# Attention rows of every second group left to VectorE in three parts, the first tap weights issued ahead of the weight loads, and the last tiles in twos

## The chip, the cores and the metric

The kernel runs on one core of a Trainium2 chip. A core has a matrix engine (TensorE; in the profile PE, with its weight loads as PEld), a vector engine (VectorE, DVE), an activation engine (ScalarE, ACT), a general engine (GpSimd, POOL) and a queue engine (SyncE, SP), each with its own instruction stream, which it runs in order. They meet through semaphores. The metric is the device time of one execution in microseconds.

## What is computed

Two things in a row, over 8 sequences of 4160 positions with 192 features, in float32. First a causal convolution whose seven taps are made per position and head by a softmax:

```python
w = np.exp(weight_gen - np.max(weight_gen, axis=-1, keepdims=True))
w = w / (np.sum(w, axis=-1, keepdims=True) + 1e-09)       # (B, S, 8 heads, 7 taps)
x_unf = x_pad[:, idx, :].reshape(B, S, K, H, group)       # the 7 last positions of each
out = np.einsum('bshk,bskhg->bshg', w, x_unf)
```

Then every position's 192 values go through a block with 1024 hidden values:

```python
h = x @ w_in
e = np.exp(h - np.max(h, axis=-1, keepdims=True))
sm = e / (np.sum(e, axis=-1, keepdims=True) + 1e-09)
solu = h * sm
ln = (solu - mean) / np.sqrt(var + 1e-06) * g_ln          # mean and var over the 1024
return (ln @ w_out).astype(np.float32)
```

## The kernel before, in words

Partition p holds a run of 260 consecutive positions, so the work is 260 **tiles**, tile t being position t of all 128 runs. Tiles are loaded in chunks (4, 8, then 16 tiles each; `starts`), and attention is made by GpSimd in **groups** of four tiles (the first four in two groups of two), 66 groups in all.

Per chunk, `softmax_taps` makes the tap weights in seven steps t0 to t6 that alternate between engines: VectorE L112 (maximum), GpSimd L114, ScalarE L118 (exponential), VectorE L120 (sum), ScalarE L122, VectorE L124 (reciprocal), GpSimd L126. For the first chunk these seven stand, in program order, behind the issues of the weights' loads (L191 to L207).

Per group, `attention` on GpSimd multiplies the seven shifted rows with the taps (L174), adds products 0 to 2 and 3 to 5 (L180), and then makes two half sums out of the four rows left (L182) into the tile `half`. VectorE adds the two halves (`last_sum`, L433, called "fin" in the order of issue), ScalarE copies 64 columns (L439).

Per two tiles, TensorE transposes (L450, "xT"), ScalarE rounds to the high part (L458, "xhi"), VectorE subtracts for the low part (L479, "xld").

Per tile the chain is: first product on TensorE (L491 and L494, "mm1") into one of three PSUM tiles `h`; VectorE's maximum (L505, "max"); ScalarE's exponential (L509, "exp"); VectorE's product h*e (L515, "solu"); ScalarE's high half in float16 (L528, "hi") and squares with their sum (L521, "sq"); VectorE's low half (L532, "lo"); a transposing DMA on SP's queue (L540, "tr"); the second product on TensorE (L580, "mm2", 24 matmuls) into `po`; ScalarE's scaled copy out (L591, "out"). "sq" and "lo" of one tile read the same `h` and are kept apart: whichever is issued first is waited for by the other. Per two or four tiles (`stat_group`) six small steps f0 to f5 (L555 to L571) make the scale of the output from the statistics.

At the start the double-precision weights are converted on VectorE and ScalarE (`float_of_double`, L241 to L260), w_in as parts a0, b and a1, then w_out as c0 to c3, whose column sums TensorE makes (L342) after ScalarE has scaled them (L334); L292 and L363 are two more small sums. The first product needs the w_in parts, the second those of w_out (L360, L385, L390).

The instruction streams are written out by `issue_order`, a planner in the program: it gives every step a cost, an engine, and a key (its tile number plus a number from the table `URGENCY`), fills the engines one step at a time, and the order in which it placed the steps is the program order. On the chip only the order remains; no time of the planner's is in it.

## Time and profile before

| | us |
|---|---|
| median of 3 runs | 1347.44 (1345.54 to 1348.4) |
| the profiled execution | 1347.67 |
| its span, first to last instruction | 1345.8 |
| TensorE / GpSimd busy | 1246.8 / 1247.7 |
| VectorE / ScalarE busy | 1210.2 / 1162.8 |
| GpSimd's last instruction ends at | 1290.4 |

Between the profiled execution's time and its span lie 1.9 us. A row of the view by stretch gives the stretch in us from the span's start, its length, and then each engine's busy time in it, with the number of instructions; after them come the granted TensorE clock (1.00 is full), the mean busy share of the DMA engines and GB/s. A row of the timeline gives start, duration, engine, line, operation, the tiles out<-in with their shapes, and in brackets how long the engine stood idle before it and for whom. A row of the groups gives line, engine, operation, tiles, shapes out<-in and count, then busy us and mean ns of one, then idle time before. A row of the waits gives who waited for whom: us in total, times, longest.

### The profile page before, as it was taken

The numbers are of one execution on the slowest core, as the hardware profiler recorded it, in microseconds if no ns is written. First come the engines' busy times: TensorE is split into PE (matmuls) and PEld (weight loads), VectorE is DVE, ScalarE is ACT, GpSimd is POOL, SyncE is SP. The second block draws the span as 40 slices with busy tenths as digits, with TensorE's granted clock in tenths as the row PEclk, the third lists the DMA queues.
The fourth block names the chain that finished last, engine by engine and source line by source line (L and its number), as shares of the span: only waits on it lengthen the run. The fifth ranks groups of instructions, "written<-read, shape, count | busy, mean of one in ns | idle before, by whom it ended". The sixth has DMA issues, their size and how long they took to land.

```text
span 1345.8 us, 25810 instructions
## 1 busy us (share of the span) xinstructions
PE 1246.8 (93%) x9900; PEld 970.8 (72%) x9900; DVE 1210.2 (90%) x1588; ACT 1162.8 (86%) x2318; POOL 1247.7 (93%) x241
## 2 busy tenths in 40 slices
PE   0588899999999999999999999999999999999997
PEld 0365677777777777777777777777777777777776
DVE  5988899999999999999999999999999999889994
ACT  3778889889898988989898998989898898988886
POOL 5989899999999999999999999999999999999930
PEclk9899999999999999999999999999999999999999
DMA  5277668797886889688797968878787877976776
GB/s 180 74 159 169 139 134 201 123 207 137 155 179 134 196 137 208 125 179 163 129 202 140 191 140 180 162 128 203 140 193 137 183 150 138 183 134 123 133 134 130
DMA packets 565307, 210.31 MB, mean 156 GB/s; under 512 B 544456, under 2 KB 545864, under 8 KB 565184
## 3 DMA queue, kind: packets, MB, share of 16 engines
q1 hardware_dynamic: 563208, 206.55, 75.7%
q10 hardware_dynamic: 1976, 2.12, 0.6%
q8 instruction: 78, 1.28, 0.4%
q14 instruction: 45, 0.37, 0.1%
HBM read 46.15 MB, written 25.56 MB: 53 GB/s over the span
## 4 chain that ended last, share of the span: by engine, by line
ACT 43%; DVE 35%; issue 11%; PE 7%; DMA 2%; POOL 1%; SPq 0%; ACTq 0%; POOLq 0%
ACT hl L528 12%; ACT e L521 12%; DVE h L515 11%; DVE hl L532 11%; ACT e L509 9%; DVE stats L505 5%; DVE a L433 4%; ACT junk L145 3%; PE po L580 3%; PE h L494 2%; ACT x_hi L458 2%; ACT ot L591 2%; DMA hlT<-hl 2%; PE h L491 1%; DVE x_lo L479 1%
## 5 line engine op out<-in xcount | busy, mean ns | idle before, releaser
L174 POOL TENSOR_TENSOR pr<-xt,wt 128x5376 f32<-128x5376 f32 (+1 forms) x66 | 631.6, 9569 | 2.7
L580 PE MATMUL po<-w_hl,hlT 128*128 128x192 f16 x6192 | 555.1, 246 | 17.3 <-ACT ot L591 12.6
L580 PEld LDWEIGHTS <-hlT 128*128 128x128 f16 x6240 | 505.9, 98 | 83.2 <-issue 75.5
L515 DVE SCALAR_TENSOR_TENSOR h<-h,row,e 128x1024 f32<-128x1024 f32 x260 | 333.8, 1285 | 19.1 <-ACT e L509 16.9
L528 ACT ACTIVATE hl<-h 128x1024 f16<-128x1024 f32 x260 | 266.0, 1029 | 98.4 <-DVE h L515 55.4
L532 DVE SCALAR_TENSOR_TENSOR hl<-h,hl 128x1024 f16<-128x1024 f32 x260 | 316.5, 1218 | 36.8 <-ACT e L521 34.4
L180 POOL TENSOR_TENSOR pr<-pr 128x2304 f32<-128x2304 f32 (+1 forms) x66 | 333.0, 5045 | 5.2
L505 DVE TENSOR_REDUCE stats<-h 128x1 f32<-128x1024 f32 x260 | 316.3, 1217 | 3.9 <-PE h L494 3.3
L509 ACT ACTIVATE e<-h,stats 128x1024 f32<-128x1024 f32 x260 | 293.3, 1128 | 16.1 <-DVE stats L505 15.5
L521 ACT ACTIVATE e<-h,stats 128x1024 f32<-128x1024 f32 x260 | 293.0, 1127 | 1.1 <-DVE hl L532 1.0
L494 PE MATMUL h<-wa_hi,x_hi 128*128 128x512 f32 x520 | 234.0, 450 | 0.0
L182 POOL TENSOR_TENSOR half<-pr 128x1536 f32<-128x1536 f32 (+1 forms) x66 | 225.8, 3421 | 5.2
L494 PE MATMUL h<-wa_lo,x_hi 128*128 128x512 f32 x520 | 206.4, 397 | 0.0
L494 PE MATMUL h<-wa_hi,x_lo 128*128 128x512 f32 x520 | 205.9, 396 | 0.0
L494 PEld LDWEIGHTS h<-wa_hi,x_hi 128*128 128x128 f32 x520 | 98.1, 189 | 107.1 <-issue 95.5
L491 PE MATMUL h<-wb_hi,x_hi 64*128 64x512 f32 x520 | 131.0, 499 | 17.1 <-DVE hl L532 11.2
L433 DVE TENSOR_REDUCE a<-half 128x768 f32<-128x1536 f32 (+1 forms) x66 | 117.2, 1776 | 0.0
L591 ACT ACTIVATE ot<-po,stats 128x192 f32<-128x192 f32 x258 | 112.4, 436 | 3.6 <-PE po L580 3.6
L494 PEld LDWEIGHTS h<-wa_hi,x_lo 128*128 128x128 f32 x520 | 98.4, 189 | 23.2
L494 PEld LDWEIGHTS h<-wa_lo,x_hi 128*128 128x128 f32 x520 | 99.0, 190 | 12.0
L491 PE MATMUL h<-wb_hi,x_lo 64*128 64x512 f32 x520 | 104.2, 395 | 0.0
L450 PE MATMUL pa<-ident,a 128*128 128x128 f32 x520 | 81.2, 278 | 23.9 <-DVE x_lo L479 13.2
(89 smaller groups left out, 1072.0 us busy)
## 6 DMA issues: line engine op xcount, KB each, us to landing
out_dram<-ot SPq DMA_DIRECT2D x65, 384.0 KB, 3.3
xt<-in_x_dram SPq DMA_DIRECT2D x30, 576.0 KB, 4.8
xt<-in_x_dram SPq DMA_DIRECT2D x30, 480.0 KB, 4.4
wt<-in_weight_gen_dram SPq DMA_DIRECT2D x15, 448.0 KB, 4.8
hlT<-hl SPq DMA_TRANSPOSE x260, 4.7
xt<-in_x_dram SPq DMA_DIRECT2D x3, 384.0 KB, 4.6
raw_a<-in_moe_w_in_dram ACTq DMA_DIRECT2D x2, 512.0 KB, 7.4
raw<-in_moe_w_out_dram ACTq DMA_DIRECT2D x1, 768.0 KB, 12.2
```

The source lines that it names most:

```text
L174: nc.gpsimd.tensor_tensor(out=window(pr, 0, [(TG * D, K), (HG, n * H), (1, HG)]), in0=window(xt, t * D, [(D, K), (HG, n * H), (1, HG)]), i ...
L180: nc.gpsimd.tensor_tensor(out=pr[:, :3], in0=pr[:, :3], in1=pr[:, 3:6], op=ALU.add)
L182: nc.gpsimd.tensor_tensor(out=half, in0=window(pr, 0, [(2 * TG * D, 2), (D, n), (1, D)]), in1=window(pr, TG * D, [(5 * TG * D, 2), (D, n), ...
L491: nc.tensor.matmul(h[:, fs], lhs[rows, 1, :], rhs[rows], start=n == 0, stop=False)
L494: nc.tensor.matmul(h[:, fs], lhs[:, 0, :], rhs[:, fs], start=False, stop=n == 2)
L505: nc.vector.tensor_reduce(stat(t, NMAX), h_of[t], axis=AX.X, op=ALU.max, negate=True)
L509: nc.scalar.activation(e, h_of[t], AF.Exp, bias=stat(t, NMAX), accum_out=stat(t, Z))
L515: nc.vector.scalar_tensor_tensor(out=h, in0=h, scalar=row(t, SCALE), in1=e, op0=ALU.mult, op1=ALU.mult, accum_out=stat(t, M))
L521: nc.scalar.activation(e_of.pop(t), h_of[t], AF.Square, bias=stat(t, M), scale=-float(FF), accum_out=stat(t, Q),)
L528: nc.scalar.activation(hl[:, 0, :], h_of[t], AF.Copy, scale=2.0**14)
L532: nc.vector.scalar_tensor_tensor(out=hl[:, 1, :], in0=h_of[t], scalar=2.0**14, in1=hl[:, 0, :], op0=ALU.mult, op1=ALU.subtract,)
L580: nc.tensor.matmul(po[:, :D], hlT[:, half * NJ + j, :], w2_hl[:, j, w, :], start=n == 0, stop=n == len(terms) - 1,)
```

## The change

Four things change in the code. (1) For a group whose number t // 4 is odd, `half` has three parts: GpSimd's first addition writes them (products 0 to 2 plus 3 to 5), the seventh product is added to the first of them in place, the addition into two halves is gone, and VectorE's `last_sum` reduces over three parts. There are 32 such groups, all of four tiles; the others are as before. `half` grows from two to three parts in both its buffers. (2) The seven tap steps of the first chunk are issued directly behind the loads of its x and taps, ahead of the weights' loads. (3) The last four tiles are attended to, and get their output scales, in twos. (4) The planner has other costs for the three-part groups, other times at which engines and data are taken to be free, one more precedence for the scaling of w_out (parts a0 and a1 are converted first), and a new table `URGENCY`, so that the order of nearly all instructions on all engines is another.

```diff
@@ def attention(xt, wt, t, n, half):
+        if half.shape[1] == 3:
+            nc.gpsimd.tensor_tensor(out=half, in0=pr[:, :3], in1=pr[:, 3:6], op=ALU.add)
+            nc.gpsimd.tensor_tensor(out=half[:, 0], in0=half[:, 0], in1=pr[:, 6], op=ALU.add)
+            return
         nc.gpsimd.tensor_tensor(out=pr[:, :3], in0=pr[:, :3], in1=pr[:, 3:6], op=ALU.add)
...
     load_x(0)
+    for step in range(TAP_STEPS):
+        softmax_taps(0, step)
     raw_a = att.tile([P, 2 * FF], I32, name="raw_a", bufs=1)
...
-
-    for step in range(TAP_STEPS):
-        softmax_taps(0, step)
...
     def stat_group(t):
-        n = 2 if t < 2 * TG else TG
+        n = 2 if t < 2 * TG or t >= RUN - TG else TG
...
     def group(t):
-        if t < TG:
+        if t < TG or t >= RUN - TG:
             return 2 if t % 2 == 0 else 0
         return TG if t % TG == 0 else 0
+
+    def parts(t):
+        return 3 if t // TG % 2 else 2
...
-        half = att.tile([P, 2, TG, D], F32, name="half", bufs=2)[:, :, :n]
+        half = att.tile([P, 3, TG, D], F32, name="half", bufs=2)[:, : parts(t), :n]
...
 URGENCY = dict(
-    a00=3.1, a01=2.3, a02=-28.9, a03=-6.5, a04=-3.6, a10=80, a11=-25.4, a12=-13, a13=-10, a14=10.4,
+    a00=-3, a01=-149.1, a02=7.4, a03=1.4, a04=4.5, a10=-41, a11=-136.7, a12=-13.9, a13=-118.7,
...
-    free = [3000, 5900, 5000, 12000, 9050]
+    free = [3000, 5600, 7700, 12000, 6200]
...
-            once(f"q{f}0", ACT, 700, part + "2")
+            once(f"q{f}0", ACT, 700, part + "2", "a02", "a12")
...
-        add("attA", t, POOL, 14990 if full else 7500, *after, ready=15000 if c == 1 else 9000)
-        add("attB", t, POOL, 3510 if full else 1800, ("attA", t), ("fin", groups[i - 2] if i > 1 else -1))
+        three = t // 4 % 2
+        add("attA", t, POOL, (9790 if three else 14990) // (1 if full else 2), *after, ready=21500 if c == 1 else 10000)
+        add("attB", t, POOL, (6950 if three else 3510) // (1 if full else 2), ("attA", t), ("fin", groups[i - 2] if i > 1 else -1))
...
-        add("fin", t, DVE, 1710 if full else 880, ("attB", t), ("xT", old + 2 if old >= 0 else -1))
+        add("fin", t, DVE, (2500 if three else 1710) // (1 if full else 2), ("attB", t), ("xT", old + 2 if old >= 0 else -1))
```

In the changed file the lines up to L174 keep their numbers; the two new additions are L181 and L182, the old two are L184 and L186; the loads are six lines lower down (L195 is L201), the weights' preparation three (L342 is L345), and the lines of the tile chain seven (L494 is L501, L521 is L528, L528 is L535).

The new table moves instructions at three places that the prediction speaks of. The first is ScalarE's stream at the start: `xt`, `raw_a` and `raw_2` are the tiles into which x, w_in and w_out are loaded, `wt` the taps, `junk` the squares of x. Before:

```order
L79 DMA xt<-in_x_dram 15x1152 x4
L195 DMA raw_a<-in_moe_w_in_dram 128x1024 x2
L202 DMA raw<-in_moe_w_out_dram 128x4x384
L206 DMA g<-in_moe_g_ln_dram 128x8x1
L118 ACTIVATE wt<-wt 128x224
L145 ACTIVATE junk,squares_x<-xt 128x1920
L122 ACTIVATE wy<-wm 128x32
```

And in the changed kernel:

```order
L79 DMA xt<-in_x_dram 15x1152 x4
L201 DMA raw_a<-in_moe_w_in_dram 128x1024
L118 ACTIVATE wt<-wt 128x224
L201 DMA raw_a<-in_moe_w_in_dram 128x1024
L122 ACTIVATE wy<-wm 128x32
L208 DMA raw<-in_moe_w_out_dram 128x4x384
L212 DMA g<-in_moe_g_ln_dram 128x8x1
```

ScalarE's two tap steps (L118, L122) now stand between the DMA issues, the second load of w_in and that of w_out behind them.

The second is TensorE's stream up to the third tile's first product (`pa` is written by the transposes, `po` by the sums over the weights, `h` by the first products; of each first product only its first row is shown here). Before:

```order
L292 MATMUL po<-sq,ones 128x3
L450 MATMUL pa<-ident,a 128x128 x4
L342 MATMUL po<-raw_a,ones 128x192 x2
L450 MATMUL pa<-ident,a 128x128 x4
L342 MATMUL po<-raw_a,ones 128x192 x2
L491 MATMUL h<-wb_hi,x_hi 128x512 x2
```

And in the changed kernel:

```order
L457 MATMUL pa<-ident,a 128x128 x4
L295 MATMUL po<-sq,ones 128x3
L457 MATMUL pa<-ident,a 128x128 x4
L345 MATMUL po<-raw_a,ones 128x192 x4
L498 MATMUL h<-wb_hi,x_hi 128x512 x2
```

Before, the sums of the first and of the second part of w_out stood ahead of the first tile's first product, in two pieces with a transpose between; now one row of four matmuls (two parts' sums) stands there, behind both transposes.

The third is ScalarE's stream in the middle of the program, tiles 170 to 172 before and 162 to 163 in the changed kernel (the numbers tell the buffers apart: an `h_` number is one tile). Before:

```order
L528 ACTIVATE hl_10506<-h_10401 128x1024
L521 ACTIVATE e_10472,stats_139<-h_10401,stats_139 128x1024
L509 ACTIVATE e_10516,stats_139<-h_10459,stats_139 128x1024
L591 ACTIVATE ot_10420<-po_10480,stats_139 128x192
L458 CAST x_hi_10534<-pa_10511 128x512
```

And in the changed kernel, the same steps seven lines higher:

```order
L535 ACTIVATE hl_10008<-h_9895 128x1024
L516 ACTIVATE e_10012,stats_139<-h_9956,stats_139 128x1024
L598 ACTIVATE ot_10028<-po_9980,stats_139 128x192
L562 ACTIVATE stats_139<-stats_139,row_7916 128x4
L528 ACTIVATE e_9969,stats_139<-h_9895,stats_139 128x1024
```

The squares of a tile (L521, now L528) stood right behind its high half and ahead of the next tile's exponential; here they stand behind the next exponential and the copy out. Both patterns occur in both programs. Of the 260 rows of the squares, 67 wait on VectorE before and 120 in the changed kernel, that is, they are issued behind the tile's low half there.

More of the change, by code (lines that the diff above doesn't have):

```diff
@@ L645 @@
 URGENCY = dict(
-    a00=3.1, a01=2.3, a02=-28.9, a03=-6.5, a04=-3.6, a10=80, a11=-25.4, a12=-13, a13=-10, a14=10.4,
-    attA=85.1, attB=2.4, b0=120.9, b1=-144.6, b2=138.3, b3=-1.5, b4=54.3, c00=-28.1, c01=85.1,
-    c02=6.8, c10=-25.3, c11=31.3, c12=-72.7, c20=99.4, c21=-5.6, c22=10.2, c30=-149.7, c31=-14.5,
-    c32=-100.3, dup=52.6, exp=-129.5, f0=8.2, f1=-120.4, f2=-71.5, f3=-118.4, f4=-66.1, f5=-45.6,
-    fin=18.4, hi=-11, lo=33, lw=18.7, lx0=10.2, lx1=-115.4, lx2=-109.1, lx3=-20.7, max=-30,
-    mm1=25.5, mm2=0.4, n0=-7.5, n1=11.8, n2=-1.8, n3=-113.6, n4=-8.6, n5=-69, n6=-123.6, od=-6.9,
-    out=-81.2, p30=22.9, p31=0.5, p4=9.7, p5=12.6, p6=11.6, p70=-10.2, p71=-8.7, p80=20.3, p81=5.9,
-    q00=7.1, q01=-5.1, q02=118.9, q10=-15.7, q11=20.7, q12=16.8, q20=100.6, q21=-95.2, q22=20.4,
-    q30=143.8, q31=81.5, q32=98.3, solu=-7.6, sq=5, t0=5.1, t1=-3.7, t2=77.9, t3=44.1, t4=-26.5,
-    t5=110.1, t6=267.2, tr=-13, v00=170.9, v01=5.1, v02=44, v03=0.2, v1=54.2, v2=58.8, v3=-12.2,
-    v4=1, v5=21.2, xT=-66.9, xhi=-46.7, xld=30,
+    a00=-3, a01=-149.1, a02=7.4, a03=1.4, a04=4.5, a10=-41, a11=-136.7, a12=-13.9, a13=-118.7,
+    a14=8, attA=78.6, attB=-30.7, b0=-73.2, b1=-107.9, b2=10.9, b3=64, b4=76.6, c00=-59.4,
+    c01=91.8, c02=-77.6, c10=-126.1, c11=133.9, c12=-2, c20=4.6, c21=-22.1, c22=-33.2, c30=-2.8,
+    c31=148.3, c32=20.6, dup=-30.2, exp=-265.5, f0=-7.8, f1=-33.1, f2=-75.4, f3=-322.6, f4=44.3,
+    f5=-45.6, fin=17.5, hi=2.4, lo=-96.1, lw=-6.9, lx0=23.5, lx1=0.2, lx2=-19.1, lx3=-15.4,
+    max=2.6, mm1=-3.4, mm2=1.7, n0=257, n1=-49.4, n2=31.3, n3=-114.7, n4=124.6, n5=-8.5, n6=12.5,
+    od=140.5, out=-181.5, p30=107.4, p31=-13.9, p4=-46, p5=84.1, p6=-11.6, p70=-18.2, p71=-102.8,
+    p80=24.2, p81=3.6, q00=2.2, q01=-34.7, q02=15.8, q10=-168.8, q11=44.9, q12=31.7, q20=-7.6,
+    q21=7.5, q22=-1.3, q30=24.6, q31=1.8, q32=-121, solu=-2.8, sq=72.9, t0=13.8, t1=28, t2=87.6,
+    t3=96.9, t4=138.5, t5=-1.5, t6=-141.4, tr=-155.6, v00=7.3, v01=168.7, v02=106.5, v03=46.2,
+    v1=11.3, v2=-84.2, v3=81.7, v4=108.9, v5=-190.2, xT=-6.4, xhi=63.8, xld=0.8,
 )
@@ L682, in issue_order @@
         w_in, size = n < 3, 512 if n < 3 else 384
-        at = (9000, 10500, 12000)[n] if w_in else 15000
+        at = (12000, 12000, 12500)[n] if w_in else 20000
         before = () if w_in else (f"{parts[n - 3]}4", "n" + {"a0": "0", "a1": "1", "b": "2"}[parts[n - 3]]) if n < 6 else ("q00",)
@@ L732, in add_norms @@
         add("v5", t, ACT, 240, ("v4", t))
-    add("v00", 0, ACT, 1800, ready=9000)
+    add("v00", 0, ACT, 1800, ready=10000)
     add_norms(0, 0)
@@ L751, in issue_order @@
             else:
-                add(f"v0{part}", t, ACT, size, ready=15000)
+                add(f"v0{part}", t, ACT, size, ready=21500)
         add_norms(c, t)
```

## The prediction

> **What bounds the kernel now.** I read the page's engine totals first, then busy time by stretch, cut where tiles 0, 16, 48, 256 and 259 begin their first product.
>
> ```profile
> PE 1246.8 (93%) x9900; PEld 970.8 (72%) x9900; DVE 1210.2 (90%) x1588; ACT 1162.8 (86%) x2318; POOL 1247.7 (93%) x241
> ...
> 45.84:138.56 92.72, 71.82 (x475) 52.81 (x474) 80.20 (x113) 73.41 (x154) 87.86 (x19) 0.91 0.63 138
> 45.84:299.99 254.15, 226.03 (x1716) 172.88 (x1716) 227.68 (x303) 217.49 (x439) 241.39 (x48) 0.97 0.73 150
> 922.57:1000.41 77.84, 75.88 (x609) 59.13 (x608) 72.26 (x94) 69.85 (x140) 76.59 (x15) 1.00 0.78 163
> 1233.49:1309.86 76.37, 75.67 (x610) 59.61 (x610) 69.50 (x90) 66.42 (x126) 56.23 (x10) 1.00 0.74 133
> 299.99:1323.30 1023.31, 1000.43 (x8013) 780.41 (x8012) 944.40 (x1217) 915.59 (x1812) 976.18 (x177) 1.00 0.79 158
> 1323.30:1345.80 22.50, 14.95 (x157) 13.34 (x156) 7.71 (x11) 10.01 (x21) 0.00 (x0) 1.00 0.48 108
> ```
>
> No single engine owns the span. In the steady part 16 tiles take 77.84 us; of these TensorE is busy 75.88, GpSimd 76.59, VectorE 72.26, ScalarE 69.85. Two engines are full at once, so I look at who really waits, in the same 16 tiles.
>
> ```profile
> DVE stats L552 <- ACT e L521: 2.5, 3, 1.1
> DVE hl L532 <- ACT e L521: 2.3, 4, 0.6
> DVE h L515 <- ACT e L509: 1.0, 2, 0.8
> ...
> 943.68 3.47 POOL L182 TENSOR_TENSOR half<-pr 128x1536 f32<-128x1536 f32 x1
> 947.62 1.77 POOL L126 TENSOR_TENSOR wt<-wt,wy 128x896 f32<-128x896 f32 x1 [0.46 <-DVE stats L552]
> 951.01 1.80 DVE L433 TENSOR_REDUCE a<-half 128x768 f32<-128x1536 f32 x1
> ```
>
> VectorE takes up a half sum 3.9 us after GpSimd has written it (947.15 to 951.01) and never idles for it; GpSimd, in turn, waits once in 16 tiles, 0.46 us, for VectorE's part of the taps. So GpSimd's own pace is 77.84 - 0.46 = 77.4 us, a hair faster than what the others make, and not what they wait for. The others pace themselves: VectorE waits 5.8 us in 16 tiles (the three rows), always for ScalarE, 4.8 of it for squares (L521), and passes the delay on to TensorE, which loses 77.84 - 75.88 = 1.96. Three levels follow for 16 tiles: TensorE's 75.9 is the floor, GpSimd's 77.4 a second floor close to the time now, and the VectorE-ScalarE exchange sets the 77.8.
>
> The start is looser: tile 48 begins at 299.99, while 48 tiles at 77.84/16 = 4.865 us after 45.84 would have brought it to 279.4. That is 20.6 us lost beside the 45.84 that pass before the first product. After the last first product begins, 22.5 us follow.
>
> **The change part by part.** *GpSimd's additions.* Prices:
>
> ```profile
> L180 POOL TENSOR_TENSOR pr<-pr 128x2304 f32<-128x2304 f32 x64 | 327.7, 5121 | 5.0
> L182 POOL TENSOR_TENSOR half<-pr 128x1536 f32<-128x1536 f32 x64 | 222.2, 3471 | 5.0
> L182 POOL TENSOR_TENSOR half<-pr 128x768 f32<-128x768 f32 x2 | 3.6, 1814 | 0.2
> L433 DVE TENSOR_REDUCE a<-half 128x768 f32<-128x1536 f32 x64 | 115.3, 1801 | 0.0
> L433 DVE TENSOR_REDUCE a<-half 128x384 f32<-128x768 f32 x2 | 1.9, 954 | 0.0
> ```
>
> A three-part group costs 5.12 + 1.81 instead of 5.12 + 3.47: 1.66 us less, 3.3 per 16 tiles, 53 us over 32 groups. That lowers GpSimd's floor from 77.4 to 74.1, under TensorE's 75.9. By itself it is worth nothing in the steady part, since nobody there waits for GpSimd; it takes a ceiling off the order. *VectorE's reduction.* 768 more elements cost 1801 - 954 = 847 ns in the trace, so three parts cost 2.65 us: 0.85 more per group, 1.7 per 16 tiles, 27 us in all, on an engine that has 5.6 us of idle time per 16 tiles, which is not free time but waiting.
>
> *The new order in the steady part* is the unknown. Busy VectorE becomes 72.26 + 1.7 = 73.96. Lower end: TensorE's 75.9 (VectorE would have to wait under 2 us). Upper end: all 5.6 idle us stay and the additions come on top, 79.5. What lies between turns on the squares: low half and squares of a tile exclude each other, and the changed order puts the low half first in 120 tiles against 67. The price of a low half that waits is
>
> ```profile
> DVE hl L532 <- ACT e L521: 34.4, 55, 2.1
> ```
>
> 0.63 us, so 53 tiles fewer spare 33 us in 16.25 chunks' worth of tiles, 2.0 per 16: 73.96 + 5.6 - 2.0 = 77.5. The longer reductions stand mostly right ahead of a low half in the new order and fill part of what that one waits anyway; I give them 0.4 and take 77.1, nearer to today's 77.84 than to either end. The stretch from tile 48 to tile 259 is 211 tiles, 13.2 sixteens: 13.2 x (77.84 - 77.1) = 9.8 us. Its last part already ran at 76.37 per 16, so I count **-8.5**; ends 13.2 x 75.9 = 1002 against 1023.3, -21, and 13.2 x 79.5 = 1049, +26.
>
> A rule of the Trainium skill speaks against my floor: its page Perfetto Trace Analysis, section Identifying the Most-Contended Engine, holds that matmul busy time does not tell how near the roofline TensorE is, and that busy weight loads do. By that reading TensorE is at 59.13 of 77.84 and VectorE's 73.96 would be the floor, 13.2 x 1.9 = 25 us lower than mine. The trace does not bear it out: in a stretch without any idle time, first product to first product takes 4.48 us with no transpose in it (the rows follow), so that 16 tiles cannot go faster than 71.7 plus eight transposes.
>
> ```profile
> 907.53 0.50 PE L491 MATMUL h<-wb_hi,x_hi 64*128 64x512 f32 x2
> ...
> 909.92 2.15 PE L580 MATMUL po<-w_hl,hlT 128*128 128x192 f16 x24
> 912.01 0.50 PE L491 MATMUL h<-wb_hi,x_hi 64*128 64x512 f32 x2
> 916.39 0.60 PE L450 MATMUL pa<-ident,a 128*128 128x128 f32 x4
> ```
>
> (Eight transposes at about 0.53, from the row's 0.60 less the overlap with the next product, make it 75.9 again.)
>
> *The first taps.* Before, GpSimd stood for 13.26 us, because VectorE's sum over the taps was queued behind a conversion that waited for its load until 12.38, and ScalarE's exponential behind five DMA issues.
>
> ```profile
> 8.86 0.39 ACT L118 ACTIVATE wt<-wt 128x224 f32<-128x224 f32 x1 [6.84 <-issue]
> 9.15 1.79 ACT L145 ACTIVATE junk<-xt 128x1920 f32<-128x1920 f32 x1
> ...
> 12.38 0.69 DVE L241 TENSOR_SCALAR h<-raw_a 128x512 int32<-128x512 int32 x1 [9.09 <-DMA raw_a<-in_moe_w_in_dram]
> ...
> 17.08 0.58 POOL L126 TENSOR_TENSOR wt<-wt,wy 128x224 f32<-128x224 f32 x1 [13.26 <-DVE wy L124]
> 17.73 4.95 POOL L174 TENSOR_TENSOR pr<-xt,wt 128x2688 f32<-128x2688 f32 x1
> ```
>
> Now the taps are ready at about 9 and x is there by 9.15 (L145 reads all of it): GpSimd begins 8.5 us earlier. Nothing else waits for GpSimd then: the first two tiles' reduction sits behind the conversions on VectorE, so what counts is VectorE. Moved with the taps: on ScalarE the second load of w_in and that of w_out are issued behind two tap steps, about 1 us later; w_in's second half is read at 21.6 and has 9 us of slack.
>
> VectorE's rows at the start, with ScalarE's scaling and TensorE's sums behind the conversions:
>
> ```profile
> 21.61 0.68 DVE L241 TENSOR_SCALAR h<-raw_a 128x512 int32<-128x512 int32 x1
> 22.33 0.69 DVE L244 TENSOR_SCALAR h<-raw_a 128x512 int32<-128x512 int32 x1
> ...
> 43.38 0.55 DVE L241 TENSOR_SCALAR h<-raw 128x384 int32<-128x384 int32 x1
> 43.96 0.56 DVE L244 TENSOR_SCALAR h<-raw 128x384 int32<-128x384 int32 x1
> ...
> 42.90 0.73 ACT L334 ACTIVATE raw_a<-h,g 128x192 f32<-128x192 f32 x2 [1.36 <-DVE h L260]
> ...
> 44.42 1.49 PE L342 MATMUL po<-raw_a,ones 128*128 128x192 f32 x4
> 45.84 0.79 PE L491 MATMUL h<-wb_hi,x_hi 64*128 64x512 f32 x2
> ```
>
> VectorE from 12.4 us on, counted off its new order: 24 conversions and sums of 512 columns at 0.60 to 0.70, 12 of 384 at 0.56, two reductions at 0.87, two low parts at 0.60, taps 1.6, small ones 0.3, 27.5 us, so the second part of w_out is converted at 39.9. ScalarE scales it (0.73), TensorE sums it (half of the 1.49), and tile 0's product begins near 41.4 instead of 45.84. Four parts are then converted by 47.4, when VectorE begins the first maximum, instead of 50.59.
>
> ```profile
> 50.59 1.21 DVE L505 TENSOR_REDUCE stats<-h 128x1 f32<-128x1024 f32 x1
> ...
> 62.40 1.25 PE L450 MATMUL pa<-ident,a 128*128 128x128 f32 x4 [9.29 <-DVE stats L552]
> 63.58 0.79 PE L491 MATMUL h<-wb_hi,x_hi 64*128 64x512 f32 x2
> 70.04 0.50 PE L491 MATMUL h<-wb_hi,x_hi 64*128 64x512 f32 x2
> ```
>
> TensorE then stands, as it did for 9.29 us before, until VectorE has reduced tiles 4 to 7 and the first tile's low half has freed an `h` for tile 2. From 47.4, VectorE has two maxima, two products, one reduction of 2.65, two operations of 1 us, some small ones and the low half to do: 12 us, 59.4, against 63.58. The fourth tile follows the second low half, near 62, where it began at 70.04 behind a second product that the new order puts later: -8. From there to tile 48 it took 299.99 - 70.04 = 230 us for 45 tiles, which at 4.865 are 219, so 11 us are lost to filling the pipeline. GpSimd, 8.5 us earlier and 1.66 shorter every second group, no longer has its part in these; I take half, 5, and get **-13**; ends 0, if the earlier tiles meet the same later waits, and -19.
>
> *The end.* Twos instead of fours let two tiles' scales be made ahead of the last two's, and the new order keeps seven instead of five second products behind the last first product, where TensorE is idle 22.5 - 14.95 = 7.5 us. Worth 0 to 2 x 2.15 = 4.3 (the L580 row above); the path there is the last tile's own chain and transpose, so **-1.5**.
>
> Sum: -13 - 8.5 - 1.5 = -23 against the profiled execution's 1347.67, which is 0.2 us from the median of 1347.44: 1324.5, forecast **1324**.
>
> **The rivals.** *VectorE becomes the pacer* (slower). The 0.85 us of each longer reduction go onto the chain VectorE-ScalarE-VectorE and no wait shrinks: 79.5 per 16, +26, start -8, no gain at the end: 1347.7 + 26 - 8 = 1366. For it: VectorE's idle time is waiting, not room. Against: fewer low halves behind squares. It decides from the point where VectorE still waits over 77.84 - 73.96 = 3.9 us in 16 tiles. *TensorE goes dense* (75.9): -21 - 19 - 4 = 1304. For it: the tap-free stretch at the end ran at 76.37. Against: VectorE at 73.96 may wait 1.9 only. *Only the start gains*, the steady 77.84 stays: 1347.7 - 13 - 1.5 = 1333. *The change does not do what it says*: the head start is eaten by the wait for `h` and the steady part stays: 1347. *VectorE is the floor and TensorE gives way*: 73.96 per 16, -21 - 25 - 19 - 4 = 1279; the dense rows above speak against it.
>
> **How the numbers follow.** Forecast 0.51, with its own range 1310 to 1338; TensorE dense 0.15; start only 0.14; VectorE as pacer 0.14; no change 0.04; below TensorE's floor 0.02. A measurement of this kernel can tell about 0.2% from no change, 2.7 us. Faster: 0.51 + 0.15 + 0.14 + 0.02 = 0.82; same 0.04; slower 0.14. The range 1300 to 1350 leaves out the pacer's case, the one below the floor and a little of the dense one, about 0.18.
>
> **What would show it.** The first L174 near 9 us and tile 0's product near 41; VectorE's reductions of 128x2304 at 2.65 us and GpSimd's second addition of 128x768 at 1.8; GpSimd now waiting for VectorE, by some 3 us per 16 tiles; 16 tiles in the middle in 76 to 78 us with TensorE still near 75.9 busy. I am wrong if 16 tiles take 78 or more with VectorE waiting as long for L528 (the squares) as before, or if the reductions cost clearly more than 2.65.

## The result, and the profile after

The changed kernel took 1365.2 us (median of four runs, 1361.4 to 1368.2) against 1347.9 us for the kernel before (four runs, 1345.5 to 1348.4): the ratio is 1.013, with an interval from 1.010 to 1.016. It is 17 us slower; forecast was 1324 us, 23 us faster. The profiled execution took 1366.46 us, its span is 1364.7 us.

Below is the page's row of engine totals for the changed kernel. Its lines stand 7 lower than before from the tile functions on, so that L440 is the old L433, L528 the old L521.

```profile
PE 1257.4 (92%) x9900; PEld 979.5 (72%) x9900; DVE 1237.2 (91%) x1592; ACT 1166.1 (85%) x2323; POOL 1195.5 (88%) x244
```

GpSimd (POOL) has 52.2 us less to do than before, and VectorE's (DVE) total is 27.0 higher. That total counts time in which two instructions overlap only once; the reductions taken by themselves add up to 32 us more, as the next rows show. TensorE (PE) shows 10.6 us more for the same 9900 products; that comes back at the end.

Next the groups of instructions of the changed kernel by shape (count, busy time, mean in ns):

```profile
L440 DVE TENSOR_REDUCE a<-half 128x768 f32<-128x2304 f32 x32 | 89.9, 2810 | 0.0
L182 POOL TENSOR_TENSOR half<-half,pr 128x768 f32<-128x768 f32 x32 | 58.4, 1825 | 2.5
L440 DVE TENSOR_REDUCE a<-half 128x768 f32<-128x1536 f32 x31 | 55.8, 1799 | 0.0
```

The reduction over three parts takes 2.81 us, 1.01 more than that over two; GpSimd's second addition takes 1.83.

Where the time went is read from busy time by stretch, cut at the first products of tiles 48 and 259. The two short rows are single stretches of 16 tiles from the middle. The columns are length, busy time of TensorE, its weight loads, VectorE, ScalarE, GpSimd, then the granted clock, the share of DMA and GB/s.

```profile
298.32:1337.16 1038.84, 1005.89 (x7990) 785.10 (x7990) 966.37 (x1217) 917.43 (x1810) 923.75 (x177) 0.99 0.79 155
619.82:695.86 76.04, 73.78 (x586) 57.24 (x586) 73.23 (x93) 69.99 (x138) 73.89 (x15) 1.00 0.84 165
853.95:936.35 82.40, 78.20 (x610) 61.00 (x610) 74.61 (x96) 69.45 (x142) 79.94 (x16) 0.96 0.82 157
1337.16:1364.70 27.54, 19.05 (x205) 17.37 (x204) 7.94 (x14) 11.96 (x28) 0.00 (x0) 0.98 0.44 104
```

Tile 48 begins 1.7 us earlier than before (298.32 against 299.99). The steady part is 15.5 us longer (1038.84 against 1023.31), and what follows the last first product is 5.0 longer (27.54 against 22.50). Together that is the span's 18.9. Before, each 16 tiles of the steady part took 77.3 to 77.9 us, all but the last 76.4. Now they take between 76.0 and 82.4. So the kernel has not become evenly slower; it has become uneven. A quick stretch flatters itself a little: the 76.04 us hold 586 TensorE instructions, the stretches around them 609 or 610, the difference being one second product of 24.

The waits over the whole run tell what is late. First the kernel before, then the changed one; the columns are total us, number of times and the longest.

```profile
DVE stats L552 <- ACT e L521: 40.3, 47, 2.2
...
PE po L580 <- ACT ot L591: 12.6, 16, 2.7
...
ACT junk L145 <- DMA xt<-in_x_dram: 6.4, 4, 2.8
...
DVE hl L532 <- ACT hl L528: 0.7, 1, 0.7
```

```profile
DVE hl L539 <- ACT e L528: 42.7, 52, 4.0
ACT junk L145 <- DMA xt<-in_x_dram: 36.2, 19, 4.8
PE po L587 <- ACT ot L598: 35.3, 32, 4.1
...
DVE hl L539 <- ACT hl L535: 17.5, 14, 3.6
...
ACT wt L118 <- POOL wt L114: 13.5, 5, 4.5
...
DVE stats L559 <- ACT e L528: 0.3, 1, 0.3
```

VectorE's waits for the squares of z (L521, now L528) fell from 34.4 + 40.3 to 42.7 + 0.3 us. Taken singly, the low half's wait for them (L532, now L539) rose from 34.4 to 42.7; what all but went is the wait of the output's statistics (L552, now L559). In their place stand waits that were small before: ScalarE stands 36 us for pieces of x (L145, the squares for the norm of x), VectorE stands for ScalarE's high half (L535; 17.5 us, before 0.7), and TensorE for the copy of the output out of its PSUM tile (L598). All in all VectorE's idle time in the steady part went from 1023.31 - 944.40 = 78.9 to 1038.84 - 966.37 = 72.5 us.

One such place, in the stretch of 82.40 us, by the timeline of SP's queue, ScalarE, VectorE and TensorE (start, duration, engine, line; in brackets the idle time before and what ended it):

```profile
893.35 0.68 SPq L90 DMA_DIRECT2D xt<-in_x_dram  x1
894.14 5.62 SPq L547 DMA_TRANSPOSE hlT<-hl  x1
899.81 0.57 SPq L90 DMA_DIRECT2D xt<-in_x_dram  x1
900.48 3.91 SPq L547 DMA_TRANSPOSE hlT<-hl  x1
904.44 0.57 SPq L90 DMA_DIRECT2D xt<-in_x_dram  x1
```

```profile
904.62 0.84 ACT L145 ACTIVATE junk<-xt 128x768 f32<-128x768 f32 x1 [3.87 <-DMA xt<-in_x_dram]
905.46 1.00 ACT L535 ACTIVATE hl<-h 128x1024 f16<-128x1024 f32 x1
...
906.50 1.23 DVE L539 SCALAR_TENSOR_TENSOR hl<-h,hl 128x1024 f16<-128x1024 f32 x1 [3.65 <-ACT hl L535]
...
907.46 0.42 ACT L598 ACTIVATE ot<-po,stats 128x192 f32<-128x192 f32 x1
...
907.92 0.32 PE L587 MATMUL po<-w_hl,hlT 128*128 128x192 f16 x1 [4.10 <-ACT ot L598]
```

The four pieces of the next x are issued on SP's queue, one behind each transposing DMA. The second piece was issued only at 899.81, behind the transpose's 5.62 us. ScalarE comes to the first squares (L145) early and stands 3.87 us for that piece; behind it in ScalarE's own order stand the high half and the output's copy, so VectorE stands 3.65 us and TensorE 4.10. The first squares read what the second piece brings, which was issued 4.81 us ahead of them. In the kernel before the pieces also stood one behind each transpose, but the squares came later, here 6.65 us behind the second piece:

```profile
912.77 0.43 SPq L90 DMA_DIRECT2D xt<-in_x_dram  x1
913.32 3.89 SPq L540 DMA_TRANSPOSE hlT<-hl  x1
917.26 0.57 SPq L90 DMA_DIRECT2D xt<-in_x_dram  x1
...
919.42 0.88 ACT L145 ACTIVATE junk<-xt 128x768 f32<-128x768 f32 x1
```

At the start the taps did move:

```profile
8.85 4.94 POOL L174 TENSOR_TENSOR pr<-xt,wt 128x2688 f32<-128x2688 f32 x1
...
42.45 0.80 PE L498 MATMUL h<-wb_hi,x_hi 64*128 64x512 f32 x2
```

GpSimd's first product (L174) begins at 8.85 instead of 17.73, and tile 0 at 42.45 instead of 45.84. The lead of 3.4 us has shrunk to 1.7 by tile 48.

### The profile page after: what moved, and what is told of

It reads as the page before. It is cut to its first block, busy times and chain, and to the rows that moved or that the text cites. A ratio compares the mean times of both kernels' runs of the same rounds, so it can differ in the third digit from the quotient of the medians.

```text
span 1364.7 us, 25947 instructions
## 1 busy us (share of the span) xinstructions
PE 1257.4 (92%) x9900; PEld 979.5 (72%) x9900; DVE 1237.2 (91%) x1592; ACT 1166.1 (85%) x2323; POOL 1195.5 (88%) x244
## 4 chain that ended last, share of the span: by engine, by line
DVE 25%; PE 24%; ACT 21%; POOL 15%; issue 10%; DMA 4%; SPq 1%; POOLq 0%; ACTq 0%; DVEq 0%
PE po L587 11%; POOL pr L174 8%; DVE hl L539 8%; PE h L501 7%; DVE h L522 7%; ACT hl L535 6%; ACT e L516 5%; ACT e L528 5%; DVE stats L512 4%; PE h L498 4%; DMA xt<-in_x_dram 4%; DVE a L440 4%; POOL half L181 2%; POOL pr L184 2%; DVE x_lo L486 1%
## 5 line engine op out<-in xcount | busy, mean ns | idle before, releaser
L174 POOL TENSOR_TENSOR pr<-xt,wt 128x5376 f32<-128x5376 f32 (+1 forms) x67 | 631.5, 9426 | 2.8
L587 PE MATMUL po<-w_hl,hlT 128*128 128x192 f16 x6192 | 563.0, 248 | 40.6 <-ACT ot L598 35.3
L587 PEld LDWEIGHTS <-hlT 128*128 128x128 f16 x6240 | 512.7, 99 | 112.7 <-issue 108.1
L539 DVE SCALAR_TENSOR_TENSOR hl<-h,hl 128x1024 f16<-128x1024 f32 x260 | 316.6, 1219 | 60.9 <-ACT e L528 42.7
L535 ACT ACTIVATE hl<-h 128x1024 f16<-128x1024 f32 x260 | 266.6, 1025 | 72.6 <-DVE h L522 54.3
L512 DVE TENSOR_REDUCE stats<-h 128x1 f32<-128x1024 f32 x260 | 316.7, 1219 | 9.0 <-PE h L501 8.7
L528 ACT ACTIVATE e<-h,stats 128x1024 f32<-128x1024 f32 x260 | 290.9, 1119 | 1.4 <-DVE hl L539 1.2
L501 PE MATMUL h<-wa_hi,x_hi 128*128 128x512 f32 x520 | 234.4, 451 | 0.0
L501 PE MATMUL h<-wa_lo,x_hi 128*128 128x512 f32 x520 | 207.1, 398 | 0.0
L501 PE MATMUL h<-wa_hi,x_lo 128*128 128x512 f32 x520 | 206.5, 397 | 0.0
L501 PEld LDWEIGHTS h<-wa_hi,x_hi 128*128 128x128 f32 x520 | 98.4, 189 | 108.0 <-issue 96.1
L184 POOL TENSOR_TENSOR pr<-pr 128x2304 f32<-128x2304 f32 (+1 forms) x35 | 169.4, 4839 | 2.7
L181 POOL TENSOR_TENSOR half<-pr 128x2304 f32<-128x2304 f32 x32 | 163.8, 5120 | 2.5
L440 DVE TENSOR_REDUCE a<-half 128x768 f32<-128x2304 f32 (+1 forms) x67 | 149.5, 2232 | 0.0
L598 ACT ACTIVATE ot<-po,stats 128x192 f32<-128x192 f32 x258 | 110.4, 428 | 12.2 <-PE po L587 11.9
L186 POOL TENSOR_TENSOR half<-pr 128x1536 f32<-128x1536 f32 (+1 forms) x35 | 115.0, 3285 | 2.7
L501 PEld LDWEIGHTS h<-wa_hi,x_lo 128*128 128x128 f32 x520 | 98.6, 190 | 23.1
L501 PEld LDWEIGHTS h<-wa_lo,x_hi 128*128 128x128 f32 x520 | 99.3, 191 | 12.0
```

Of the source, the lines that this page charges most:

```text
L174: nc.gpsimd.tensor_tensor(out=window(pr, 0, [(TG * D, K), (HG, n * H), (1, HG)]), in0=window(xt, t * D, [(D, K), (HG, n * H), (1, HG)]), i ...
L181: nc.gpsimd.tensor_tensor(out=half, in0=pr[:, :3], in1=pr[:, 3:6], op=ALU.add)
L184: nc.gpsimd.tensor_tensor(out=pr[:, :3], in0=pr[:, :3], in1=pr[:, 3:6], op=ALU.add)
L440: nc.vector.tensor_reduce(columns(t)[:, :, :D], half.rearrange("p j t d -> p t d j"), axis=AX.X, op=ALU.add)
L501: nc.tensor.matmul(h[:, fs], lhs[:, 0, :], rhs[:, fs], start=False, stop=n == 2)
L512: nc.vector.tensor_reduce(stat(t, NMAX), h_of[t], axis=AX.X, op=ALU.max, negate=True)
```

## The experiments

Four theories were tried against each other. *Loads*: the pieces of x stand behind transposes and hold ScalarE, and all behind it. *Reduction*: VectorE's 1.01 us more per three-part group is what costs. *Taps*: GpSimd hands the tap weights over too late, behind a long product. *GpSimd floor*: the prediction's picture that GpSimd's work holds the kernel before near its pace, so that relief for it gives the order room.

The table gives all the runs that are told below; steps are us per 16 tiles from tile 48 to tile 256, in the profiled execution, as the mean of 13 and as the lowest and highest. Each ratio is to the kernel before as it was measured again beside that run (medians of 1346.6 to 1348.4 us).

| run | median us | ratio to before (interval) | tile 48 at | steps: mean (low to high) |
|---|---|---|---|---|
| before | 1347.9 | | 299.99 | 77.68 (76.4 to 77.9) |
| changed | 1365.2 | 1.0130 (1.0101 to 1.0160) | 298.32 | 78.88 (76.0 to 82.4) |
| e1 loads together | 1340.3 | 0.9944 (0.9929 to 0.9959) | 288.64 | 77.55 (74.5 to 83.4) |
| e2 two of three parts read | 1354.1 | 1.0042 (1.0027 to 1.0058) | 294.96 | 78.46 (74.8 to 82.4) |
| e3 old order, three parts | 1373.4 | 1.0191 (1.0173 to 1.0208) | 304.88 | 79.24 (77.9 to 79.5) |
| e4 old order, taps first | 1344.9 | 0.9978 (0.9969 to 0.9987) | 297.25 | 77.69 (76.4 to 77.9) |
| e5 e1 + later taps | 1340.2 | 0.9940 (0.9924 to 0.9957) | 289.49 | 77.63 (75.2 to 79.7) |
| e6 e5 with two parts | 1370.1 | 1.0166 (1.0151 to 1.0181) | 287.81 | 79.86 (75.1 to 83.9) |
| e7 changed + later taps | 1380.7 | 1.0242 (1.0226 to 1.0257) | 299.31 | 79.90 (76.1 to 83.5) |
| e8 e1, two of three read | 1333.5 | 0.9881 (0.9864 to 0.9897) | 287.59 | 77.23 (73.9 to 84.3) |
| e9 e1, TensorE less | 1340.1 | 0.9936 (0.9921 to 0.9950) | 287.78 | 77.59 (74.3 to 83.6) |
| e10 e1, ScalarE less | 1338.2 | 0.9920 (0.9905 to 0.9935) | 286.94 | 77.51 (73.9 to 84.1) |
| e11 e1, end in fours | 1340.0 | 0.9939 (0.9924 to 0.9953) | 288.99 | 77.55 (74.8 to 83.4) |
| e12 old order, GpSimd less | 1348.2 | 1.0008 (0.9999 to 1.0018) | 300.43 | 77.71 (76.4 to 77.9) |
| e13 e8 and e9 together | 1329.3 | 0.9869 (0.9854 to 0.9884) | 287.47 | 76.84 (73.0 to 84.0) |
| e14 e1, half of the low parts off VectorE | 1433.9 | 1.0656 (1.0635 to 1.0677) | 298.13 | 84.46 (78.2 to 96.1) |

**e1: the pieces of x together.** The changed kernel, with the four pieces of a load issued right behind each other:

```diff
-    for op, t in issue_order(RUN, starts, group, stat_group, LOADS):
+    for op, t in pieces_together(issue_order(RUN, starts, group, stat_group, LOADS)):
+def pieces_together(order):
+    out = []
+    for op, t in order:
+        if op in ("lx1", "lx2", "lx3"):
+            continue
+        out.append((op, t))
+        if op == "lx0":
+            out += [(f"lx{n}", t) for n in range(1, 4)]
+    return out
```

> The changed kernel with one move: the second to fourth piece of each x load are issued right behind the first on SP's queue, not behind two or three transposes; every other stream keeps its order. Theory of the loads (ScalarE's squares of x, L145, stand for a piece that left its queue late, 26 us between tiles 48 and 259, and all else behind them): L145's waits fall from 36 us to under 10 and the time from 1365 to 1335 to 1345. Theory of the reduction (VectorE's 32 longer reductions go onto the path one to one): 1362 to 1368, whatever happens to L145. Theory of the taps (GpSimd, ScalarE and VectorE hand the taps of a chunk to each other late): 1360 to 1367.

1340.3 us: 25 us faster than the changed kernel, and faster than the kernel before. A load's row in SP's queue (four pieces at once) and the waits of e1:

```profile
871.28 2.57 SPq L90 DMA_DIRECT2D xt<-in_x_dram  x4
...
ACT wt L118 <- POOL wt L114: 20.6, 6, 5.0
...
DVE hl L539 <- ACT hl L535: 5.0, 9, 1.2
...
ACT junk L145 <- DMA xt<-in_x_dram: 2.9, 3, 1.2
```

ScalarE's wait for x falls from 36.2 to 2.9 us, VectorE's for the high half from 17.5 to 5.0. Tile 48 now begins at 288.64, 9.7 us earlier than in the changed kernel: the start, too, had been held by these loads. The loads theory holds, for 25 us. Against the kernel before, the profiled execution of e1 is 8 us shorter, and that comes from the start: tile 48 begins 11.4 us earlier, the steady part (1021.67 us, before 1023.31) is 1.6 us shorter, and the 27.5 us behind the last first product are 5 us longer.

**e2: the longer reduction made shorter.** In the changed kernel VectorE reads only two of the three parts of a group; the third part of these groups' attention sum is then left out.

```diff
-            columns(t)[:, :, :D], half.rearrange("p j t d -> p t d j"), axis=AX.X, op=ALU.add
+            columns(t)[:, :, :D], half[:, :2].rearrange("p j t d -> p t d j"), axis=AX.X, op=ALU.add
```

> The changed kernel, but VectorE's reduction reads only two of the three parts in every second group (the third part of the attention's sum is left out of the result; GpSimd still makes it). VectorE has 32 x 1.0 = 32 us less to do, all orders and GpSimd's work are kept. Theory of the reduction: 1333 to 1342. Theory of the loads and theory of the taps: VectorE had idle time behind ScalarE anyway, 1357 to 1365.

1354.1 us: VectorE has 27 us less to do, and 11 us come out. That lies between the ranges of the theories: in the changed order the longer reductions are a cause, but the smaller one.

**e3 and e4: one part of the change each, in the old order.** The kernel before, with three parts in every second group (e3), or with only the first taps moved ahead of the weights' loads (e4).

```diff
+        if half.shape[1] == 3:
+            nc.gpsimd.tensor_tensor(out=half, in0=pr[:, :3], in1=pr[:, 3:6], op=ALU.add)
+            nc.gpsimd.tensor_tensor(out=half[:, 0], in0=half[:, 0], in1=pr[:, 6], op=ALU.add)
+            return
...
-        half = att.tile([P, 2, TG, D], F32, name="half", bufs=2)[:, :, :n]
+        half = att.tile([P, 3, TG, D], F32, name="half", bufs=2)[:, : 3 if t // TG % 2 else 2, :n]
```

> The kernel before with only the three parts in every second group: GpSimd 53 us less, VectorE 32 us more, all orders those of before. Theory of the reduction: 16 tiles take 77.8 + 2.0, 1370 to 1382. If the old order has room on VectorE (it waited 5.8 us in 16 tiles, the longer reductions partly ahead of such waits): 1345 to 1360. Faster than 1345 only if GpSimd had been the bound of before, which its trace does not show.

> The kernel before with only the first chunk's seven tap steps issued ahead of the weights' loads. GpSimd's first product starts near 9 us instead of 17.7. All theories: VectorE's conversions, not GpSimd, lead to the first tile, so that tile 0 moves by under 1 us and the time stays within 1343 to 1348; the prediction's price of the start (-13 in all) would need the new order as well.

e3 took 1373.4 us. Each 16 tiles take 1.56 us more than before, and hold two of the longer reductions, 2.02 us: three quarters of VectorE's addition comes out as time. GpSimd's relief brings nothing there, as e12 shows below. e4 took 1344.9 us: tile 0 begins at 42.81, 3.0 us earlier where under 1 was expected, and these 3.0 us reach the end nearly whole (2.8), while the steady part is the same to 0.01 us per 16 tiles.

**e12: is GpSimd a floor of the kernel before?** e3 with VectorE reading two of the three parts (the same part left out as in e2): VectorE then does what it did before, GpSimd 52 us less.

> Base: e3_three_in_old_order (the kernel before with three parts in every second group, 1373.4 us). VectorE reads only two of the three parts, so part of the attention sum is left out: VectorE then has as much to do as before, GpSimd 53 us less. If GpSimd's work held the kernel before, 15 to 40 us faster than it: 1308 to 1332. If the exchange between VectorE and ScalarE sets the pace, as the chain of the kernel before says (ScalarE 43%, VectorE 35%, GpSimd 1%), no change: 1345 to 1350. And then the 26 us of e3 are the longer reductions' alone.

1348.2 us, the same as before; the interval ends at 1.0018. A stretch of 16 tiles in e12, the same stretch in e3, and the two chains that ended last (before, then e12):

```profile
922.57:1000.41 77.84, 75.88 (x609) 59.12 (x610) 72.28 (x93) 69.87 (x140) 73.33 (x15) 1.00 0.78 164
```

```profile
923.00:1002.30 79.30, 75.83 (x611) 59.10 (x609) 74.27 (x94) 69.93 (x140) 73.10 (x15) 1.00 0.77 160
```

```profile
ACT 43%; DVE 35%; issue 11%; PE 7%; DMA 2%; POOL 1%; SPq 0%; ACTq 0%; POOLq 0%
```

```profile
ACT 43%; DVE 34%; issue 11%; PE 9%; DMA 2%; POOL 1%; SPq 0%; ACTq 0%; POOLq 0%
```

GpSimd's 76.59 us per 16 tiles fall to 73.33, and the stretch takes 77.84 us as before. A GpSimd that is 98% busy and on 1% of the chain was no bound in the old order. The 25 us of e3 over e12 are therefore the longer reductions alone.

**e5 and e7: the later tap steps.** In e1 three of the thirteen stretches still take 79.9 to 83.4 us, the others 76.4 in the mean. In the slowest, GpSimd is late with the tap weights (GpSimd's rows, then what waited, in e1):

```profile
870.66 9.71 POOL L174 TENSOR_TENSOR pr<-xt,wt 128x5376 f32<-128x5376 f32 x1
880.45 5.10 POOL L181 TENSOR_TENSOR half<-pr 128x2304 f32<-128x2304 f32 x1
885.63 1.84 POOL L182 TENSOR_TENSOR half<-half,pr 128x768 f32<-128x768 f32 x1
887.43 1.76 POOL L114 TENSOR_TENSOR wt<-wt,wm 128x896 f32<-128x896 f32 x1
...
889.22 0.95 ACT L118 ACTIVATE wt<-wt 128x896 f32<-128x896 f32 x1 [5.02 <-POOL wt L114]
...
892.54 1.82 PE L587 MATMUL po<-w_hl,hlT 128*128 128x192 f16 x14 [4.33 <-ACT ot L598]
```

e5 takes e1 and moves the exponential, the sum, its copy, the reciprocal and the last product of the taps back in the order, past those of about one and a half to three tiles; e7 does this to the changed kernel, without e1's edit.

```diff
+def taps_later(order):
+    by = dict(t2=24, t3=36, t4=36, t5=36, t6=48)
+    def place(item):
+        n, (op, t) = item
+        return n + by[op] + 0.5 if op in by and t >= 36 else n
+    return [step for _, step in sorted(enumerate(order), key=place)]
```

> The changed kernel with two repairs of its written order: the four pieces of each x load together (as in e1_pieces, which took 1340.3), and each chunk's later tap steps (exponential, sum, its copy, reciprocal, last product) 24 to 48 entries later in the order of all steps, about one and a half to three tiles. Taps theory: the late stretches left in e1_pieces (80.57, 79.93 and 83.39 us per 16 tiles against 76.6 in its quiet ones) come from the exponential L118, which waits 5 us for GpSimd's L114 behind a first product L174; with it moved those three come down to about 76.6, together 14 us, so 1326 (1321 to 1332), and the waits of L118 for L114 fall from 20.6 us to under 5. Reduction theory: the 2.8 us reduction on VectorE makes these stretches late; then nothing changes much, 1337 to 1342.

> The changed kernel with the later tap steps moved as in e5_pieces_and_taps, the x loads left in pieces. If the two hold-ups add: 14 us off 1365, so 1348 to 1355. If the taps are late only because the queue of loads makes ScalarE late, nothing: 1360 to 1367. If the taps are the root of both, 1335 to 1342.

e5 took 1340.2 us, the same as e1. Of its waits:

```profile
PE po L587 <- ACT ot L598: 25.1, 38, 2.2
...
ACT wt L118 <- POOL wt L114: 4.5, 1, 4.5
```

The waits of L118 for L114 did go (from 20.6 to 4.5 us), and the slow stretches did come down (83.4 to 78.9); but the quick ones went up from 76.4 to 77.3, and the mean step stayed (77.55 and 77.63). The taps theory's gain did not come. The move also made new waits, though (GpSimd's for VectorE's maximum, L114 for L112, rose from 1.0 to 12.6 us), so what the old wait cost by itself stays open. e7 took 1380.7 us, 15 us more than the changed kernel, where each theory expected a gain or none. GpSimd's waits for VectorE's maximum (L114 for L112) rose from 6.7 to 37.1 us in it. Moving some steps later moves them against all that the other engines do, and the sum of two repairs was no guide.

**e6: two parts in the repaired order.** e5 with every group in two parts.

```diff
-        return 3 if t // TG % 2 else 2
+        return 2
```

> The order of e5_pieces_and_taps, instruction by instruction, but every group left to VectorE in two parts, so that GpSimd does 53 us more and VectorE 27 us less; the result is the same. If GpSimd paces the repaired order (its work per 16 tiles is 77.4 us with two parts against 74.1 with two and three in turn), the steps go from about 76.6 back to 77.4 or more: 10 to 20 us slower than e5, 1336 to 1346. If the longer reduction costs more than GpSimd's relief brings, as in e3_three_in_old_order, it is 5 to 15 us faster than e5, 1311 to 1322.

1370.1 us, 30 us more than e5 and beyond both expectations; of the two, the one in which GpSimd paces had the sign right. The trace of e6 says why (a row of its waits, then its chain):

```profile
DVE a L440 <- POOL half L186: 42.0, 21, 6.3
```

```profile
POOL 73%; DVE 9%; issue 8%; ACT 7%; PE 2%; DMA 0%; POOLq 0%; SPq 0%; DVEq 0%; ACTq 0%
```

VectorE stands 42 us for half sums, a wait that the lists of e5 and of the kernel before don't have. GpSimd is busy for 1245 of the 1262 us from its first product to its end at 1270.6, and 97 us follow, where 55 followed in the kernel before (1345.8 - 1290.4). So in the new order GpSimd with two parts is the bound, and the third part takes that bound away.

With e3 this gives a square of four: two parts in the old order 1348, three parts in it 1373, two parts in the new one (repaired) 1370, three parts in it 1340. Each order fits the split it was made for, and the other one costs 26 or 30 us: in the old order by VectorE's longer reductions (e12), in the new one by GpSimd's work (e6).

**e8, e9, e10, e13: what holds e1 at 1340.** Relief for one engine at a time: e8 for VectorE (e2's edit, with the same part left out), e9 for TensorE (one of the twelve products with the first matrix left out on odd tiles), e10 for ScalarE (the squares of x over half of each piece), e13 for VectorE and TensorE.

```diff
+                if n == 1 and fs.start and t % 2:
+                    continue
...
-                r1 = r0 + TC // 4
+                r1 = r0 + TC // 8
```

> Base: e1_pieces (the changed kernel with the x loads together, 1340.3 us). VectorE's reduction of a three-part group reads only two of the three parts, so that part of the attention sum is left out; VectorE has 31 us less to do, spread evenly. If VectorE paces the repaired order, most of that comes out: 1311 to 1320. If TensorE paces it (busy 986.9 of the 1008.4 us from tile 48 to tile 256), 1335 to 1341. If no single engine does and the hand-overs between them count, about a third to a half: 1325 to 1332.

> Base: e1_pieces. On every odd tile one of the twelve products of the first matrix is left out (second half, low part of the weights), 130 instructions at 0.235 us from start to start: TensorE has 30.6 us less to do. If TensorE paces: 1310 to 1316. If VectorE paces: 1336 to 1341. If the hand-overs count: 1322 to 1332.

> Base: e1_pieces. ScalarE's squares of x take half of each piece (the norm of x is then of half its values), some 26 us less work for ScalarE, in bursts once per 16 tiles. If ScalarE is on the chain at those places: 1318 to 1330. If TensorE or VectorE alone paces: 1337 to 1341.

> Base: e1_pieces with both reliefs, that of e8 (VectorE 27 us less, 1333.5) and that of e9 (TensorE 30.6 us less, 1340.1): if several engines bound the repaired order side by side, the two together bring more than their sum of 7: 1316 to 1327. If the stretches in which GpSimd is late bound it, 1331 to 1335.

Relief of 26 us for VectorE gave 7 (1333.5); 25 for TensorE, by its totals, nothing (1340.1); 14 for ScalarE, by its totals, 2 (1338.2); VectorE's and TensorE's together 11 (1329.3). The times of e8 and e13 lie between the ranges that were expected. By these medians the two together bring more than the sum of both, 7; by the ratios in the table they bring 10 us against 8.5 and 1, which is no difference beyond the intervals. GpSimd got no relief in this order; more work for it is e6. So in the repaired order relief for none of the three engines brings much alone; VectorE's brings most. A piece of e9's chain from a quick stretch shows it (start, duration, what the chain passes through; in e9 the lines from L512 on stand two lower, so L514 is the maximum, L524 and L541 the normalised product and the low half):

```profile
1024.56 0.14 DVE h L524
1024.70 1.08 DVE stats L514
1025.78 1.72 DVE a L440
1027.49 1.13 DVE hl L541
1028.62 0.49 DVE h L524
```

With TensorE relieved, the chain goes from VectorE's instruction to VectorE's next, the reduction L440 among them. And all the gain of e13 lies in the quick stretches: the ten beside the slow three fell from 76.4 to 75.2 us in the mean, the slow three went from 81.3 to 82.3. In e8 TensorE has become a floor in places: in its last stretch of 16 tiles (the first row below) TensorE is never idle. The second row is the slowest stretch of e13.

```profile
1216.38:1291.61 75.23, 75.23 (x610) 58.89 (x610) 67.07 (x88) 65.17 (x124) 16.09 (x6) 1.00 0.69 132
```

```profile
826.95:910.95 84.00, 76.76 (x601) 59.65 (x600) 73.11 (x97) 70.05 (x142) 83.05 (x17) 0.96 0.75 156
```

With TensorE's work cut as well (e13) the stretch in the first row took 74.16 us. In the second row GpSimd is busy for 83.05 of 84.00 us. What makes the slow stretches slow is not the work of VectorE and TensorE; that it is GpSimd's lateness there is argued from these rows and not shown, since e5 took the wait for it away without gain.

**e11: the end in fours again.** e1 with the last four tiles as one group, for the attention rows and for the statistics.

```diff
-        n = 2 if t < 2 * TG or t >= RUN - TG else TG
+        n = 2 if t < 2 * TG else TG
...
-        if t < TG or t >= RUN - TG:
+        if t < TG:
```

> Base: e1_pieces, with the last four tiles as one group again, for the attention rows and for the statistics. The prediction held the twos at the end worth 1.5 us: then this takes 1341.5 to 1343.5. If they are worth nothing or cost, 1337 to 1340.5.

1340.0 us against 1340.3: no difference.

**e14: work from VectorE to ScalarE.** e1 with `VECTOR_PAIRS = 2`, so that for every second pair of tiles TensorE and ScalarE make the low part of x; the order is planned anew with it.

> Base: e1_pieces, result unchanged: for every second pair of tiles the low part of x is made by TensorE and ScalarE and not by VectorE (VectorE some 40 us less, ScalarE some 30 more, TensorE some 15 more); the order of all steps is planned anew with it. If VectorE's work paces the repaired order and ScalarE has the room: 1325 to 1337, faster than e1. If the exchange of ScalarE and VectorE paces, ScalarE's share takes back what VectorE gives: 1340 to 1360.

1433.9 us, far beyond both expectations, with steps from 78.2 to 96.1 us and GpSimd waiting 42 us for its half-sum buffers (L181 for L440). The table of urgencies was made for the other split of work; with the same table, the planner's order for this one is bad. It says nothing on how much work VectorE should have.

The version that beats both kernels is e1, with e5 and e11 level: 1340.3 us, 0.56% under the kernel before.

## Why the prediction was wrong, point by point

**What bounds the kernel: right in the main.** That nobody waited for GpSimd was read rightly, and its additions were priced at nothing by themselves; e12 shows that for the old order (52 us less, no gain). The chain of waits of the kernel before (ScalarE 43%, VectorE 35%, GpSimd 1%), which the prediction did not show, says it in one row. "It takes a ceiling off the order" came true only where the order is the new one: with two parts there VectorE waits 42 us for GpSimd, and the run takes 30 us more (e6).

**The reduction: mechanism right, size off.** Forecast 2.65 us, measured 2.81. The prediction took the price of 768 more elements from a row with half as many results (128x384, also of two parts), 0.85 us; a third part to each of the same 768 results cost 1.01. The sum over the 32 reductions is 32 us, not 27. That VectorE's total rose by 27.0 all the same is a coincidence, since it counts overlapping time once; with the same reductions in the old order (e3) it rose by 31.5.

**The steady part: the step that failed.** The prediction priced the new order by one term: 53 tiles fewer in which the low half stands behind the squares, at 0.63 us each, "spare 33 us", and it put new waits at nothing. Both parts failed. The low half's waits for the squares rose from 34.4 us in 55 times to 42.7 in 52: fewer tiles have this order, but each wait is longer. VectorE's waits for the squares did fall by 31.7 us, but by luck near the 33: it is the statistics (L552) that stopped waiting, 40.3 us before, and the prediction had not priced them.

The second half weighs more. The step looked at one pair of instructions and did not ask what else had come closer together: ScalarE's squares of x now stand so close behind the loads, which are queued behind transposes of 3.9 to 5.6 us, that ScalarE waits 36 us for them. e1 puts a price on it: 25 us of the run. The kernel before had a row that gave warning, ScalarE's own wait for x, 6.4 us in 4 times, the longest 2.8; it was not looked at. Of the 33 us forecast, VectorE's idle time in the steady part lost 6.4 (78.9 to 72.5) in the changed kernel. With the loads together it lost 22.7 (to 56.2 in e1), which there pays for the longer reductions and little more. The forecast of 77.1 us per 16 tiles became 78.8 (13.2 sixteens: +15.5 us and not -8.5), inside the ends given (-21 and +26).

**"The longer reductions ... fill part of what that one waits anyway; I give them 0.4": right in kind, too small in the new order.** The 0.4 is what is covered by waits, of 1.7 us per 16 tiles. In the old order 1.56 of 2.02 us came out as time (e3), so that 0.46 were covered. In the changed order the relief of e2 took only 0.42 off the mean step (78.88 to 78.46), in the repaired one that of e8 0.32, so that some 1.6 were covered. The price of the same 1.01 us thus depends on how many other waits cover it. Over the run it still made 11 us by the medians (e2); 3.4 us of it lie ahead of tile 48.

**The start: mechanism right, then lost.** The taps were ready and L174 began at 8.85 (forecast near 9). Tile 0 came at 42.45 (forecast 41.4), the fourth tile at 66.6 (forecast 62). Of the forecast 13 us at tile 48, 1.7 were left. With the loads together it is 11.4 (288.64 against 299.99), so the estimate was near, and what took it was again the loads, in the filling of the pipeline. The part of it that belongs to the taps' place alone is e4's 3 us.

**The end: wrong, and worth nothing.** Forecast -1.5, measured +5.0 after the last first product. Eight second products lie behind it instead of six (the prediction said seven instead of five), 2 x 2.15 = 4.3 us that had lain ahead of it, so by this reckoning the true change is about +0.7. e11 shows no difference for twos or fours.

**The rivals.** The rival "VectorE becomes the pacer" gave 1366 us, and 1365 was measured; but its picture, 79.5 us in every 16 tiles, is not that of the changed kernel (76.0 to 82.4). It is that of e3: 79.2, close to the price that the rival named, where three parts are put into the old order. So its number agreed by luck, for another reason: 25 us from loads and some 11 from the reduction, against what the new order saves elsewhere. The chance for "slower" was 0.14, and 1365 lies outside the range of 1300 to 1350. One new wait per 16 tiles, at the longest that the kernel before shows for x (2.8 us), would have added 13.2 x 2.8 = 37 us to the forecast; a range that reached for it would have gone to 1361.

**The floor of TensorE.** e9 says that TensorE's work does not hold the repaired order: 25 us less of it changed nothing. But the prediction's floor of 75.9 us is there, a little lower: in e8 the row above has TensorE busy for all of 75.23 us, and cutting its work (e13) brought that stretch to 74.16. The Trainium skill, page Perfetto Trace Analysis, section Identifying the Most-Contended Engine, judges TensorE's room by its weight loads and not by matmul time. e9 agrees with that and the row of e8 does not: weight loads take 58.89 us of its 75.23. The gain that this reading promised in the prediction (VectorE's 73.96 us as the floor) did not come in any run: the mean step of e1 is 77.55, and 76.84 with both engines relieved (e13).

## What to carry to other kernels

When an order is written anew, list every pair of producer and consumer whose distance has shrunk, the loads with all that is queued ahead of them on their queue first, and price those waits beside the ones that went. An engine's busy share, even 98%, does not make it the bound. Its share of the chain that ended last is nearer, but one chain is not all of them: GpSimd had 24% of it in e1 and 3% in e5, at the same time of 1340 us. A run with its work cut settles it, and for that order only, since the same GpSimd work that nobody waited for in the old order held up the new one. A split of work and an order that were made for each other are one change: taken singly, each half of this one cost 26 to 30 us.
